# Attention plus SwiGLU on one core: odd output tiles paired into one group of seven products, output groups side by side, two weight sums later

## The chip, the cores and the metric

The kernel runs on one core of a Trainium2 chip. The metric is device time in microseconds (us) from the first to the last instruction of an execution. The kernel before takes 407.28 us (median of three runs, 407.09 to 407.64). A profiled execution of it has a span of 405.0 us; a profile's span is not a timed run, so below spans are compared with spans and times with times. A **slot** is the time from the start of one matmul to the start of the next when nothing is waited for; a **hole** is what a start comes later than its slot. The **ramp** is what runs before the first group of the first output stage, the **tail** what runs from the start of the last product to the end.

## The reference, cut to what matters

```python
# q, k, v: (8, 12, 448, 64) float32; w_gate, w_val: (768, 1536); w_out: (1536, 768)
scores = scale * np.matmul(q, k.transpose(0, 1, 3, 2)) - np.log(S)
attn = 1.0 / (1.0 + np.exp(-scores))                 # a sigmoid, no softmax
attn_out = np.matmul(attn, v)
x = attn_out.transpose(0, 2, 1, 3).reshape(B * S, H * D)     # (3584, 768)
g = x @ w_gate
silu = g * (1.0 / (1.0 + np.exp(-g)))
val = x @ w_val
out = silu * val @ w_out                                     # (3584, 768)
```

## The kernel before

The eight batches go through the feed-forward part in four pairs, `pb` = 0 to 3 (`LAST` is 3). Each pair has a first-layer stage, which makes twelve tiles `hT` (hidden channels by tokens), and an output stage, which multiplies them with `w_out`. A pair has 896 tokens, seven output tiles of 128 (`m` = 0 to 6). In tiles 0 to 5, tile `g` and tile `g + 3` form **group** `g`. A group is calculated in the manner of Strassen: seven products of six matmuls instead of eight, paid for with sums of the inputs (`S`, made on VectorE from `hT`) and of the weights (`w_sum` for the output layer, `fast_w` for the first). Tile 6 has no partner and takes the ordinary 24 matmuls. `double` is the same trick for two channel tiles of the first layer; half of pair 2's first layer and all of pair 3's use it.

A group has two PSUM banks (pieces of the memory in which TensorE collects its results). A "snap" copies a bank, scaled, to the output tile while the bank goes on collecting; a "put" adds a bank to what the output tile holds. Each product is numbered as in the code; the order is 1, 2, 6, 5, 7, 3, 4.

```python
def make_sums(most):
    for _ in range(min(most, len(sumq))):
        pb, i, f, kind = sumq.pop(0)
        ...                                            # S sums on VectorE, 128x384
        nc.vector.tensor_tensor(out=t, in0=a, in1=b, op=op)
...
def ffn2_group(pb, g):                                 # tiles g and g+3
    D = Banked("o")                                    # two PSUM banks
    ...
    mm(1, 0, True, False)                              # product 1 into bank 0
    snap(0, o1, 0)                                     # VectorE
    mm(2, 1, True, True)
    put(1, o1, 0)
    ...
    mm(6, 0, False, False)                             # bank 0 goes on: needs the snap done
    snap(0, o1, 1)
    mm(5, 1, True, False)                              # bank 1 anew: needs the put done
    o2 = osp.tile([128, DM], FP32, tag="osb", name="osb")
    snap(1, o2, 1)
    mm(7, 0, False, False)
    put(0, o2, 1)
    ...
    mm(3, 1, False, True)
    put(1, o1, 1)
    mm(4, 0, False, True)
    if not end:
        store((nc.sync, nc.sync), pb, g, o1, both)
        snap(0, o2, 0)
        store((nc.sync, nc.sync), pb, g + 3, o2, both)
        return
    ...
def ffn2(pb, m):                                       # one tile alone: 24 matmuls of 128x384
    ...
# order of the work of a pair
    extra = {
        (LAST - 1, 0): ((1, 2), (1, 4)), (LAST, 0): ((3, 3), (3, 1)), (LAST, 2): ((3, 2), (3, 4)),
    }.get((pb, f), ())                                 # fast_w sums inside `double`
    ...
    o_units = [(0.0, make_sums, (99,)), (FU2, ffn2, (pb, C - 1))]      # the odd tile comes first
    if pb == 0:
        ts = [(0.0, w_sum, (s, kind)) for s in range(2) for kind in (3, 2, 1, 4)]
        o_units += ts[:4] + [(FU2, ffn2, (pb, 0))] + ts[4:7] + [(FU2, ffn2, (pb, 3))] + ts[7:]
    for g in range(1 if pb == 0 else 0, 3):
        o_units.append((FU3, ffn2_group, (pb, g)))
```

Matmuls of the groups have line L571 in the kernel before, those of the odd tile L629, those of `double` L437. The snap is L582, the put L588, the sum S L530, `fast_w` L384 and `w_sum` L498. L460 is the addition on VectorE by which `double` empties a bank.

## Time and profile before

| | before |
|---|---|
| time, median of 3 runs | 407.28 us |
| span of the profile | 405.0 us |
| TensorE busy | 392.5 us, 97%, 3140 matmuls |
| VectorE, ScalarE, GpSimd busy | 66%, 56%, 23% |
| holes in the places that the change touches (worked out below) | 1.83 us |

An engine's timeline lists groups of like instructions: start and duration in us, engine and line, operation, output<-inputs, sizes, count; a bracket holds the idle time before them and what ended it. The prediction shows TensorE's side of three holes. Here is VectorE's side of two of them. First, beside the first group of the first output stage:

```profile
112.85 1.00 DVE L498 TENSOR_TENSOR ramp_a<-wo,ramp_a 128x1152 f16<-128x1152 f16 x1
113.77 0.55 DVE L582 TENSOR_SCALAR osb<-ps_D 128x384 f32<-128x384 f32 x1
```

The weight sum of 1.00 us stands ahead of the snap L582, and TensorE's product 6 waits for that snap. Second, the same timeline at the begin of the first `double`:

```profile
281.22 0.75 DVE L384 TENSOR_TENSOR stg_a<-wg,stg_a 128x1152 f16<-128x1152 f16 x1
281.89 1.15 DVE L460 TENSOR_TENSOR small<-ps_D,snap 128x448 f32<-128x448 f32 x2
```

The first line is a weight sum that stands ahead of L460, which releases a bank. A reader who only looks at VectorE's share of 66% would say that it has time enough. It does, but in both pairs of lines it works in the order of the program, and a sum that nobody wants yet delays an eviction that TensorE does want.

### The profile page before, as it was taken

The numbers are of one execution on the slowest core, as the hardware profiler recorded it, in microseconds if no ns is written. First come the engines' busy times: TensorE is split into PE (matmuls) and PEld (weight loads), VectorE is DVE, ScalarE is ACT, GpSimd is POOL, SyncE is SP. The second block draws the span as 40 slices with busy tenths as digits, with TensorE's granted clock in tenths as the row PEclk, the third lists the DMA queues.
The fourth block names the chain that finished last, engine by engine and source line by source line (L and its number), as shares of the span: only waits on it lengthen the run. The fifth ranks groups of instructions, "written<-read, shape, count | busy, mean of one in ns | idle before, by whom it ended". The sixth has DMA issues, their size and how long they took to land.

```text
span 405.0 us, 7990 instructions
## 1 busy us (share of the span) xinstructions
PE 392.5 (97%) x3140; PEld 203.8 (50%) x3140; DVE 266.5 (66%) x508; ACT 226.9 (56%) x355; POOL 93.7 (23%) x121
## 2 busy tenths in 40 slices
PE   6799999999999999999999999999999999999995
PEld 3444544445555444444455554444555655555563
DVE  3737556678765555567764566889786558777753
ACT  5965885744444777777764547776650035666100
POOL 4528041424222232232200120000006950000000
PEclk9999999999999999999999999999999999999999
DMA  8999989899869997778717697000001440000135
GB/s 275 245 251 249 241 189 209 166 168 237 148 187 253 241 245 160 160 159 160 160 24 189 144 248 103 2 2 1 2 0 40 121 113 0 1 2 0 40 91 143
DMA packets 65284, 54.38 MB, mean 134 GB/s; under 512 B 35744, under 2 KB 61440, under 8 KB 65248
## 3 DMA queue, kind: packets, MB, share of 16 engines
q1 hardware_dynamic: 49744, 38.22, 39.3%
q0 software_dynamic: 15072, 15.34, 23.0%
q8 instruction: 24, 0.39, 0.4%
q10 hardware_dynamic: 432, 0.33, 0.3%
q14 instruction: 12, 0.10, 0.1%
HBM read 47.19 MB, written 11.01 MB: 144 GB/s over the span
## 4 chain that ended last, share of the span: by engine, by line
PE 90%; DVE 4%; DMA 3%; ACT 1%; issue 1%; SPq 0%; POOL 0%; DVEq 0%; ACTq 0%
PE ps_D L314 34%; PE ps_D L571 18%; PE ps_D L437 15%; PE ps_D L240 8%; PE ps_D L273 8%; PE ps_D L629 6%; DMA v<-in_v_dram 2%; DMA st<-in_q_dram 1%; DVE t L336 1%; DVE xT L293 1%; DVE xT L288 0%; PE ps_D L210 0%; ACT small L467 0%; DVE stg_a L384 0%; ACT snap L447 0%
## 5 line engine op out<-in xcount | busy, mean ns | idle before, releaser
L259 ACT ACTIVATE pt_a<-ps_D 128x896 f16<-128x896 f32 x148 | 127.2, 920 | 55.3 <-PE ps_D L240 49.2
L314 PE MATMUL ps_D<-xT,wg 128*128 128x448 f16 x360 | 79.4, 353 | 0.6 <-DVE t L336 0.5
L314 PE MATMUL ps_D<-xT,wv 128*128 128x448 f16 x360 | 78.9, 352 | 0.0
L191 POOL CAST c<-stg_a 128x896 bf16<-128x896 f32 x40 | 37.5, 945 | 130.8 <-DMA stg_a<-in_q_dram 118.4
L336 DVE TENSOR_TENSOR t<-ps_D,s 128x448 f16<-128x448 f32 x60 | 37.4, 623 | 43.7 <-ACT s L334 42.6
L314 PEld LDWEIGHTS <-wg 128*128 128x128 f16 x360 | 32.3, 98 | 39.4 <-issue 13.6
L314 PEld LDWEIGHTS <-wv 128*128 128x128 f16 x360 | 35.1, 98 | 33.0 <-issue 0.4
L334 ACT ACTIVATE s<-ps_D 128x448 f16<-128x448 f32 x60 | 33.1, 551 | 26.5 <-PE ps_D L314 26.5
L240 PE MATMUL ps_D<-T,T 64*64 64x448 bf16 x644 | 44.1, 357 | 2.1 <-DVE T L216 1.2
L447 ACT ACTIVATE snap<-ps_D 128x448 f32<-128x448 f32 x54 | 28.0, 542 | 31.8 <-DVE osb L582 20.7
L340 DVE SCALAR_TENSOR_TENSOR hT<-ps_D,t 128x448 f16<-128x448 f32 x60 | 37.5, 625 | 6.3
L273 PE MATMUL ps_D<-pt_a,v 64*64 64x448 f16 x672 | 35.9, 349 | 0.6 <-DMA v<-in_v_dram 0.6
L582 DVE TENSOR_SCALAR osb<-ps_D 128x384 f32<-128x384 f32 x43 | 24.0, 557 | 18.7 <-PE ps_D L571 18.5
L571 PEld LDWEIGHTS <-S 128*128 128x128 f16 x264 | 25.8, 98 | 17.7 <-issue 0.7
L571 PE MATMUL ps_D<-ramp_a,S 128*128 128x384 f16 x198 | 34.0, 326 | 0.5 <-DVE osb L582 0.5
L588 DVE SCALAR_TENSOR_TENSOR osb<-ps_D,osb 128x384 f32<-128x384 f32 x33 | 18.4, 557 | 13.4 <-PE ps_D L571 13.3
L240 PEld LDWEIGHTS <-T 64*64 64x64 bf16 x644 | 14.9, 105 | 24.5 <-issue 17.8
L273 PEld LDWEIGHTS <-v 64*64 64x64 f16 x672 | 19.4, 107 | 13.4 <-DMA v<-in_v_dram 1.0
L571 PEld LDWEIGHTS <-hT 128*128 128x128 f16 x198 | 19.0, 98 | 14.0 <-issue 1.8
L288 DVE CAST xT<-ps_D 128x448 f16<-128x448 f32 x21 | 13.1, 624 | 19.1 <-PE ps_D L273 17.4
L629 PE MATMUL ps_D<-wo,hT 128*128 128x384 f16 x144 | 24.6, 326 | 0.2 <-DVE hT L482 0.2
L437 PE MATMUL ps_D<-xS,wv 128*128 128x448 f16 x108 | 23.4, 352 | 0.3 <-DVE small L460 0.2
(98 smaller groups left out, 426.7 us busy)
## 6 DMA issues: line engine op xcount, KB each, us to landing
out_dram<-osb SPq DMA_DIRECT2D x52, 192.0 KB, 3.0
stg_a<-in_q_dram SPq DMA_DIRECT2D x18, 448.0 KB, 5.2
stg_a<-in_k_dram SPq DMA_DIRECT2D x18, 448.0 KB, 6.0
v<-in_v_dram POOLq DMA_DIRECT2D x24, 224.0 KB, 6.0
wg<-in_moe_w_gate_dram POOLq DMA_DIRECT2D x4, 576.0 KB, 11.9
wv<-in_moe_w_val_dram POOLq DMA_DIRECT2D x4, 576.0 KB, 12.9
wo<-in_moe_w_out_dram POOLq DMA_DIRECT2D x4, 576.0 KB, 10.1
stg_a<-in_q_dram POOLq DMA_DIRECT2D x3, 448.0 KB, 13.8
```

The lines of the kernel that those rows point to most:

```text
L191: eng.tensor_copy(out=t.rearrange("p c h d -> p h c d"), in_=st.rearrange("p h (c d) -> p h c d", c=C))
L240: nc.tensor.matmul(out=sc[w * 64:(w + 1) * 64, h2, :S], lhsT=kt[r, w * 64:(w + 1) * 64], rhs=qt[r, :, w * 64:(w + 1) * 64], start=True, st ...
L259: nc.scalar.activation(out=pt, in_=sc[:, :, :S], func=SIGM, bias=sbias, scale=qkscale)
L273: nc.tensor.matmul(out=P[g:g + 64, h2, :S], lhsT=vt[r, h2, c * D:(c + 1) * D], rhs=pt[r, h2, :], start=(c == 0), stop=(c == C - 1),)
L314: nc.tensor.matmul(out=D.t[:, i, :S], lhsT=(wg16, wv16)[i][f // FW][:, pr, cs], rhs=xT[(b, pr)], start=(pr == 0), stop=(pr == NP - 1),),
L334: D.read(nc.scalar.activation(out=s16, in_=D.t[:, 0, :S], func=SIGM), 0)
L336: D.read(nc.vector.tensor_tensor(out=t1, in0=D.t[:, 0, :S], in1=s16, op=MULT), 0)
L340: nc.vector.scalar_tensor_tensor(out=hT[(b // 2, f)][:, b % 2, :], in0=D.t[:, 1, :S], scalar=hsc(b // 2), in1=t1, op0=MULT, op1=MULT),
L437: nc.tensor.matmul(out=D.t[:, bank, :S], lhsT=W(f, j), rhs=X(j), start=(start and j == 0), stop=(stop and j == JT - 1), skip_group_check=True,
L447: D.read(nc.scalar.mul(out=o, in_=D.t[:, bank, :S], mul=scale), bank)
L571: nc.tensor.matmul(out=D.t[:, bank, :hw], lhsT=l, rhs=B_(i), start=(first and i == 0), stop=(i == HF - 1), skip_group_check=True,),
L629: nc.tensor.matmul(out=D.t[:, half, :hw], lhsT=h[:, m * 128:(m + 1) * 128], rhs=wo16[f // FW][:, f % FW, half * hw:(half + 1) * hw], start ...
```

## The change

Its intent has four parts.

- The odd tiles of pairs 2 and 3 become one more group of seven products (`g == 3`), run in the last stage: 42 matmuls instead of 48. ScalarE keeps pair 2's last 128 tokens of each `hT` (`keep_rest`, 12 copies), and GpSimd makes the sums (`rest_sums`, 24 of them).
- With the odd tile gone from the head of the stage, nothing would cover the sums S. So groups 0 and 1 of pairs 2 and 3 run side by side, product by product, with their first snap on ScalarE.
- Two weight sums come later: `w_sum(1, 4)` behind the put of product 2 of the first group, `fast_w(0, 4)` into the first `double`. `fast_w(1, 4)` moves on by one `double`.
- The S sums are sorted by kind, and the first tile's store comes right after product 3's put.

```diff
     def make_sums(most):
+        if most > NF:
+            sumq.sort(key=lambda s: s[3] % 3 if s[3] < 4 else 3)
...
+    def keep_rest():
+        for f in range(NF):
+            nc.scalar.copy(out=rest_h(f), in_=hT[(LAST - 1, f)].rearrange("p b s -> p (b s)")[:, (C - 1) * 128:])
+
+    def rest_sums():
+        G.tensor_copy(out=held[:, :1], in_=hS[(LAST, 4, FW - 1)][:, :1])
+        of = lambda f: hT[(LAST, f)].rearrange("p b s -> p (b s)")[:, (C - 1) * 128:]
+        for kind in (1, 2, 3, 4):
+            for i in range(HF):
...
+                G.tensor_tensor(out=t, in0=a, in1=b, op=op)
+
-    def ffn2_group(pb, g):
+    def ffn2_group(pb, g, act=False):
...
+        rows = ((pb, g), (pb, g + 3)) if g < 3 else ((LAST - 1, C - 1), (LAST, C - 1))
...
         mm(1, 0, True, False)
-        snap(0, o1, 0)
+        if act:
+            D.read(nc.scalar.mul(out=o1[:, :hw], in_=D.t[:, 0, :hw], mul=1.0 / hsc(pb)), 0)
+        else:
+            snap(0, o1, 0)
+        yield
         mm(2, 1, True, True)
         put(1, o1, 0)
...
         mm(3, 1, False, True)
         put(1, o1, 1)
+        if not end:
+            store((nc.sync, nc.sync), *rows[0], o1, both)
+        yield
         mm(4, 0, False, True)
         if not end:
-            store((nc.sync, nc.sync), pb, g, o1, both)
             snap(0, o2, 0)
...
+    def ffn2_groups(pb, gs, extra=()):
+        gens = [ffn2_group(pb, g, len(gs) > 1) for g in gs]
+        extra = list(extra)
+        while gens:
+            gens = [g for g in gens if next(g, g) is not g]
+            if extra:
+                extra.pop(0)()
...
-                (LAST - 1, 0): ((1, 2), (1, 4)), (LAST, 0): ((3, 3), (3, 1)), (LAST, 2): ((3, 2), (3, 4)),
+                (LAST - 1, 0): ((0, 4), (1, 2)), (LAST - 1, 2): ((1, 4),), (LAST, 0): ((3, 3), (3, 1)), (LAST, 2): ((3, 2), (3, 4)),
...
-        o_units = [(0.0, make_sums, (99,)), (FU2, ffn2, (pb, C - 1))]
+        o_units = [(0.0, make_sums, (99,))]
+        if pb < LAST - 1:
+            o_units.append((FU2, ffn2, (pb, C - 1)))
...
+        ex = {(0, 1): (lambda: None, lambda: w_sum(1, 4)), (LAST - 1, 0): (keep_rest,)}
+        gs = {0: ((1,), (2,)), LAST - 1: ((0, 1), (2,)), LAST: ((0, 1), (3,), (2,))}.get(pb, ((0,), (1,), (2,)))
+        for g in gs:
+            o_units.append((FU3 * len(g), ffn2_groups, (pb, g, ex.get((pb, g[0]), ()))))
```

More of the change, by code (lines that the diff above doesn't have):

```diff
@@ L541, in store_half, with h_of @@
         eng.dma_start(out=d, in_=osb[w * 64:(w + 1) * 64, cols])
-    def ffn2_group(pb, g):
+    rest_h = lambda i: pt_f[:, 5 * JT * FW * 128 + i * 128:5 * JT * FW * 128 + (i + 1) * 128]
+    rest_s = lambda i: half_of(stg_a)[:, i * 128:(i + 1) * 128]
+    def keep_rest():
[6 more added lines that the diff above has]
+            for i in range(HF):
+                f = i // FW * 2 * FW + i % FW
+                hS[("rest", kind, i)] = t = rest_s((kind - 1) * HF + i)
+                a, b, op = {
+                    1: (of(f), of(f + FW), ADD), 2: (rest_s(i), rest_h(f), SUB), 3: (rest_h(f), of(f), SUB),
+                    4: (rest_h(f + FW), rest_s(HF + i), SUB),
+                }[kind]
+                G.tensor_tensor(out=t, in0=a, in1=b, op=op)
+    def ffn2_group(pb, g, act=False):
         D = Banked("o")
         cs = slice(g * 128, (g + 1) * 128)
-        def h_of(f, m):
+        rows = ((pb, g), (pb, g + 3)) if g < 3 else ((LAST - 1, C - 1), (LAST, C - 1))
+        def h_of(f, r):
             f1 = lambda i: i // FW * 2 * FW + i % FW + f
+            p, m = rows[r]
+            if p != pb:
+                return lambda i: (rest_h(f1(i)), None)
             return lambda i: (hT[(pb, f1(i))].rearrange("p b s -> p (b s)")[:, m * 128:(m + 1) * 128], f1(i))
         def s_of(kind):
+            if g == 3:
+                return lambda i: (hS[("rest", kind, i)], None)
             return lambda i: (hS[(pb, kind, i)][:, cs], None)
@@ L561, in ffn2_group @@
         prods = {
-            1: (h_of(0, g), w_of(0, 0)), 2: (h_of(FW, g), w_of(1, 0)), 3: (s_of(4), w_of(1, 1)),
-            4: (h_of(FW, g + 3), t_of(4)), 5: (s_of(1), t_of(1)), 6: (s_of(2), t_of(2)), 7: (s_of(3), t_of(3)),
+            1: (h_of(0, 0), w_of(0, 0)), 2: (h_of(FW, 0), w_of(1, 0)), 3: (s_of(4), w_of(1, 1)),
+            4: (h_of(FW, 1), t_of(4)), 5: (s_of(1), t_of(1)), 6: (s_of(2), t_of(2)), 7: (s_of(3), t_of(3)),
         }
@@ L597, in ffn2_group @@
         if end:
-            store((nc.sync, nc.sync), pb, g, o1, lo)
+            store((nc.sync, nc.sync), *rows[0], o1, lo)
+        yield
         mm(6, 0, False, False)
         snap(0, o1, 1)
+        yield
         mm(5, 1, True, False)
@@ L603, in ffn2_group @@
         snap(1, o2, 1)
+        yield
         mm(7, 0, False, False)
@@ L606, in ffn2_group @@
         if end:
-            store((nc.sync, nc.sync), pb, g + 3, o2, hi)
+            store((nc.sync, nc.sync), *rows[1], o2, hi)
+        yield
         mm(3, 1, False, True)
         put(1, o1, 1)
+        if not end:
+            store((nc.sync, nc.sync), *rows[0], o1, both)
+        yield
         mm(4, 0, False, True)
         if not end:
-            store((nc.sync, nc.sync), pb, g, o1, both)
             snap(0, o2, 0)
-            store((nc.sync, nc.sync), pb, g + 3, o2, both)
+            store((nc.sync, nc.sync), *rows[1], o2, both)
             return
-        store((nc.sync, nc.scalar), pb, g, o1, hi)
+        store((nc.sync, nc.scalar), *rows[0], o1, hi)
         oe = stg_tile().rearrange("p a b -> p (a b)")
         snap(0, oe, 0)
-        store((nc.sync, nc.scalar), pb, g + 3, oe, lo)
+        store((nc.sync, nc.scalar), *rows[1], oe, lo)
+    def ffn2_groups(pb, gs, extra=()):
[5 more added lines that the diff above has]
+                extra.pop(0)()
     def ffn2(pb, m):
@@ L668 @@
             tt += FU4
-        o_units = [(0.0, make_sums, (99,)), (FU2, ffn2, (pb, C - 1))]
+        o_units = [(0.0, make_sums, (99,))]
+        if pb < LAST - 1:
+            o_units.append((FU2, ffn2, (pb, C - 1)))
         if pb == 0:
             ts = [(0.0, w_sum, (s, kind)) for s in range(2) for kind in (3, 2, 1, 4)]
-            o_units += ts[:4] + [(FU2, ffn2, (pb, 0))] + ts[4:7] + [(FU2, ffn2, (pb, 3))] + ts[7:]
-        for g in range(1 if pb == 0 else 0, 3):
-            o_units.append((FU3, ffn2_group, (pb, g)))
+            o_units += ts[:4] + [(FU2, ffn2, (pb, 0))] + ts[4:7] + [(FU2, ffn2, (pb, 3))]
+        ex = {(0, 1): (lambda: None, lambda: w_sum(1, 4)), (LAST - 1, 0): (keep_rest,)}
+        gs = {0: ((1,), (2,)), LAST - 1: ((0, 1), (2,)), LAST: ((0, 1), (3,), (2,))}.get(pb, ((0,), (1,), (2,)))
+        for g in gs:
+            o_units.append((FU3 * len(g), ffn2_groups, (pb, g, ex.get((pb, g[0]), ()))))
         units += o_units
@@ L899 @@
             xs2 = [f for j in range(NJ) for f in x_sums(LAST - 1, j)]
-            w2 = [lambda a=a: fast_w(*a) for a in ((1, 3), (1, 1), (0, 3), (0, 1), (0, 2), (0, 4))]
+            w2 = [lambda a=a: fast_w(*a) for a in ((1, 3), (1, 1), (0, 3), (0, 1), (0, 2))]
             h = NF // 2
@@ L904 @@
                 (-2, h + 5, xs2[6:9]), (-1, h, xs2[9:]), (-1, h + 2, w2[2:3]), (-1, h + 3, w2[3:4]),
-                (-1, h + 4, w2[4:5]), (-1, h + 5, w2[5:]),
+                (-1, h + 4, w2[4:]),
             ):
@@ L914 @@
             early_w(2)
+        if fn is make_sums and (LAST, 4, FW - 1) in hS and ("rest", 1, 0) not in hS:
+            rest_sums()
 _INS = ['q', 'k', 'v', 'moe_w_gate', 'moe_w_val', 'moe_w_out']
```

## The prediction

> **What bounds the kernel now.** I read the page first: busy shares and the chain that ended last.
>
> ```profile
> PE 392.5 (97%) x3140; PEld 203.8 (50%) x3140; DVE 266.5 (66%) x508; ACT 226.9 (56%) x355; POOL 93.7 (23%) x121
> ...
> PE 90%; DVE 4%; DMA 3%; ACT 1%; issue 1%; SPq 0%; POOL 0%; DVEq 0%; ACTq 0%
> ```
>
> TensorE is busy for 97% of a 405.0 us span and carries 90% of the chain; no other engine passes 66%. So the time is the sum of matmul slots plus the few holes between them. A matmul taken away pays its slot, a hole pays its length, and work on VectorE, ScalarE or GpSimd costs nothing unless it opens a hole. Next I cut the span into stages (columns: stretch, its length, then busy us and instruction count per engine, clock, DMA):
>
> ```profile
> 279.00:303.20 24.20, 23.89 (x126) 12.18 (x125) 19.65 (x43) 14.77 (x30) 0.00 (x0) 1.00 0.01 1
> 303.20:307.70 4.50, 4.29 (x27) 2.27 (x25) 3.27 (x10) 0.75 (x2) 0.99 (x2) 1.00 0.00 0
> 307.70:328.20 20.50, 20.50 (x128) 12.35 (x127) 11.70 (x21) 0.49 (x1) 20.26 (x23) 1.00 0.37 97
> ...
> 375.80:379.70 3.90, 3.90 (x26) 2.35 (x24) 3.28 (x10) 0.76 (x2) 0.00 (x0) 1.00 0.01 4
> 379.70:400.40 20.70, 20.68 (x128) 12.23 (x125) 11.72 (x21) 0.49 (x1) 0.00 (x0) 1.00 0.41 107
> ```
>
> The two odd output tiles (24 matmuls each) are the stretches that begin at 303.2 and 375.8; the three groups of seven products follow each. The groups are full. The 303.2 stretch lasts 4.50 where its twin takes 3.90, so it holds a hole. VectorE and ScalarE are light there (11.7 and 0.5 us in 20.5), which is the room that the change uses. Holes then come from the timeline of TensorE (start, length, instruction; the bracket is idle time and its releaser):
>
> ```profile
> 111.77 2.12 PE L571 MATMUL ps_D<-wo,hT 128*128 128x384 f16 x12
> ...
> 114.37 3.09 PE L571 MATMUL ps_D<-ramp_a,S 128*128 128x384 f16 x18 [0.47 <-DVE osb L582]
> ```
> ```profile
> 281.04 1.30 PE L437 MATMUL ps_D<-xS,stg_a 128*128 128x448 f16 x6
> 282.56 1.29 PE L437 MATMUL ps_D<-xS,wv 128*128 128x448 f16 x6 [0.22 <-DVE small L460]
> 283.69 1.30 PE L437 MATMUL ps_D<-xS,stg_a 128*128 128x448 f16 x6
> ```
> ```profile
> 303.24 0.81 PE L629 MATMUL ps_D<-wo,hT 128*128 128x384 f16 x4
> 304.26 3.59 PE L629 MATMUL ps_D<-wo,hT 128*128 128x384 f16 x20 [0.21 <-DVE hT L482]
> ```
>
> Durations overlap (modelled ends), so I use start to start: undisturbed groups give 126 matmuls in 20.49 us, that is 0.1626 us per 128x384 matmul, and six 128x448 matmuls take 1.14 us. By that measure the holes are 114.37 − 111.77 − 12×0.1626 = 0.65; 282.56 − 281.04 − 1.14 = 0.38, followed by 285.08 − 283.69 − 1.14 = 0.25 on a ScalarE snap that the same delay made late; and 304.26 − 303.24 − 4×0.1626 = 0.37 us.
>
> **What the Trainium skill says.** "TensorE: Matmul & The Clock Gate", section "Wait — 56ns, not 53.3ns?", gives N ÷ 2.4 GHz plus about 2.5 ns from start to start on a warm array: 162.5 ns for N = 384. The trace agrees: 162.6 ns. "Perfetto Trace Analysis", section "Identifying the Most-Contended Engine", warns that matmul busy share is no measure of distance from the roofline. Here it bears on the method: I use the gaps between starts, not the 97%. "SBUF — State Buffer", section "SBUF: two separate sides", says that a VectorE operation with two SBUF inputs and a GpSimd operation that reads SBUF exclude each other: the later one blocks. The trace agrees:
>
> ```profile
> 103.27 0.98 POOL L191 CAST c<-stg_a 128x896 bf16<-128x896 f32 x1 [1.40 <-DMA stg_a<-in_k_dram]
> ```
> ```profile
> 103.37 1.48 DVE L498 TENSOR_TENSOR ramp_a<-wo 128x1152 f16<-128x1152 f16 x1
> 104.78 0.75 DVE L498 TENSOR_TENSOR ramp_a<-wo,ramp_a 128x1152 f16<-128x1152 f16 x1
> ```
>
> The sum that began 0.10 us after the cast took 1.48 us instead of 0.75: almost exactly the rest of the cast (0.88) more.
>
> **The change, part by part.**
>
> (A) Six fewer matmuls. The two odd tiles, 2×24 = 48 matmuls of 128x384, become one group of 7×6 = 42. Saved: 6×0.1626 = 0.98 us.
>
> (B) The 0.37 us hole at 304.26. The old odd tile needed hT_4, written by the last pair just before, as its fifth matmul. The side-by-side groups start with 12 matmuls that need older tiles only; hT_4 is the 14th, 13×0.1626 = 2.1 us after 303.24. VectorE delivers it by about 304.2. Saved: 0.37.
>
> (C) One of the two weight sums, (0,4), leaves the end of the ordinary stage and goes behind the two L460 additions on VectorE. Before, its 0.75 us run ended at 281.97 and L460 started at 281.89. Now L460 can start at about 281.2, its first half ends near 281.8, and product 5 may begin on time at 282.18. The ScalarE chain (snap, two silu, snap) starts on the heels of L460. In later pairs the needed snap ends about 3.24 us after the start of product 6 and is read at 3.40; here I expect it at 3.4, so about 0.05 is left. Saved: 0.38 + 0.25 − 0.05 = about 0.6.
>
> (D) The other sum, (1,4) of the output weights, at 112.85 to 113.85, stood ahead of the group's first snap. It moves behind the put of product 2. The snap then runs at about 112.95 to 113.50 and product 6 starts on time at 113.73: 0.65 gained. But the sum now runs from about 114.45 to 115.2, and the snap of product 6 behind it ends at about 115.76, while product 7 wants that bank at 113.73 + 12×0.1626 = 115.68. About 0.15 comes back as a small wait. Net 0.5.
>
> (E) Added, meant to be hidden. 12 copies of 128x128 on ScalarE (estimate from its 0.49 us for 384 and 0.54 for 448 columns: about 0.28 each, 3.4 us) in a stretch of 20 us where it is idle. GpSimd gets 24 sums of 128x128: 0.91 us for 384 columns and 1.03 for 448 extrapolate to about 0.44, or 0.23 by their start-to-start spacing, so 5.5 to 10.6 us. It can do four before the last pair ends, the rest from about 377.2, and is done by 386 at worst. In the old clock, the first of them is wanted at 375.84 + 96×0.1626 = 391.4. VectorE swaps two half-tile copies for seven group evictions of 0.56 us. All off the path.
>
> (F) Side by side. The 24 matmuls of products 1 and 2 last 3.9 us, just what the odd tile lasted; so the six sums on VectorE (377.06 to 379.25 in the last stage) still end before product 6 at 379.74. The first snap is on ScalarE, so it does not queue behind those sums. Each later step has 12 matmuls (1.95 us) against two evictions (1.12 us). Gain and cost: none.
>
> Sum: 0.98 + 0.37 + 0.6 + 0.5 = 2.45 us.
>
> **Rivals.** *GpSimd blocks the last VectorE sums.* The six sums and the 24 GpSimd ones now run at the same time, both reading SBUF. If they alternate, six steps of 0.36 + 0.3 to 0.44 end at 381.2 to 382.0 instead of 379.25. The put of product 2 behind them then ends at 381.8 to 382.6, while product 5 wants its bank at 375.84 + 36×0.1626 = 381.69. That opens a hole of 0.1 to 0.9 us. For it: the pair of lines above. Against: GpSimd waits for the same last hT, and its operations are short. I take 0.2.
>
> *A wait for output buffers.* Four buffers of 128x768 serve four tiles at once. The group after the pair writes its first half into the buffer whose store was issued in the sixth step. In the trace the second half's store lands 2.8 us after an issue that lies 0.52 after the eviction's end at 314.31, so 3.35 us. From the start of the stage: eviction ends at 66×0.1626 + 0.19 + 0.56 = 11.5, landing 14.85; the snap wants it at 90×0.1626 + 0.19 = 14.82 and has until about 15.0 before product 6 feels it. On the edge, twice. I take 0.1 in all; a slower landing of 0.5 us would cost 0.7 in all.
>
> *The gains are lost elsewhere.* If earlier matmuls only met later ones waiting for data, (C) and (D) would give nothing and about 1.3 us would be left. Against: from 129 to 279 TensorE is busy for 149.5 of 150.0 us and waits for no load. *VectorE or ScalarE as the new bound*: in the stage views they are at 57% and below 20%; this would cost microseconds, but I see no place for it.
>
> **Range and chances.** 2.45 − 0.2 − 0.1 = 2.15, so 407.28 − 2.15 = 405.1 us. If everything hides, 404.7; with (D) fully repaid (0.5 less) and 0.6 of new holes, 406.1. I add the scatter of the runs, 0.3 each way, on the good side. So 404.3 to 406.2 holds 8 in 10. Two per cent is 8.1 us: no part of the change is a quarter of it. Faster by over 2%: 0.01; within: 0.98; slower: 0.01.
>
> **What would show it.** (A) Matmuls with 384 columns fall in number by 6; the last stage is 28 products of six, at 0.1626 us each, without holes. (B) No hole in the first 24 matmuls of the output stage near 303, which lasts 126×0.1626 = 20.5 us in all. (C) Product 5 of the first pair starts 1.14 us after product 6. (D) Product 6 of the first group follows product 1 by 1.95 us, then a wait of up to 0.2 before product 7. (E) TensorE never waits for GpSimd. (F) TensorE waits at product 6 or product 5 of the last side-by-side groups, if the rival of the blocked sums is right; at product 6 of the group after them, with VectorE idle before its snap, if the buffers are. The prediction is wrong if such a wait passes 1 us, or if the span falls by under 1 us though the matmuls are gone.

## The result, and the profile after

| | before | changed |
|---|---|---|
| median of 6 runs | 407.12 us (406.81 to 407.64) | 404.6 us (403.98 to 406.96) |
| ratio, 95% interval | | 0.9944 (0.9919 to 0.997) |
| span of the profile | 405.0 us | 402.4 us |
| mean granted TensorE clock in it | 0.998 | 0.999 |

A ratio here and below is the mean time of one kernel's fast runs over the mean time of the other's fast runs of the same rounds, so it is not quite the ratio of the medians in the table. The interval lies below 1.

Busy shares and chain shares on the page of the changed kernel:

```profile
PE 391.4 (97%) x3134; PEld 203.8 (51%) x3134; DVE 269.4 (67%) x509; ACT 230.5 (57%) x369; POOL 106.0 (26%) x146
...
PE 94%; DMA 3%; DVE 1%; ACT 1%; issue 0%; SPq 0%; POOL 0%; DVEq 0%; ACTq 0%
```

TensorE has six matmuls less, and its share of the chain of waits rises from 90% to 94%, while VectorE's falls from 4% to 1%: what went was waiting on VectorE. The places of the old holes on TensorE's timeline (group matmuls are L599 in this kernel):

```profile
112.20 2.12 PE L599 MATMUL ps_D<-wo,hT 128*128 128x384 f16 x12
114.16 3.09 PE L599 MATMUL ps_D<-ramp_a,S 128*128 128x384 f16 x18
117.08 1.14 PE L599 MATMUL ps_D<-wo,S 128*128 128x384 f16 x6
...
280.83 1.30 PE L437 MATMUL ps_D<-xS,stg_a 128*128 128x448 f16 x6
281.97 1.30 PE L437 MATMUL ps_D<-xS,wv 128*128 128x448 f16 x6
...
284.24 1.30 PE L437 MATMUL ps_D<-xS,wv 128*128 128x448 f16 x6
...
302.40 4.06 PE L599 MATMUL ps_D<-wo,hT 128*128 128x384 f16 x24
306.30 6.01 PE L599 MATMUL ps_D<-ramp_a,S 128*128 128x384 f16 x36
```

No line carries a bracket. The starts say the same: 114.16 − 112.20 = 1.96 for twelve matmuls, 117.08 − 114.16 = 2.92 for eighteen, 281.97 − 280.83 = 1.14 for six of 448 columns and 284.24 − 281.97 = 2.27 for the next twelve, 306.30 − 302.40 = 3.90 for 24. Each is the undisturbed slot. Two stretches of stages (length, then busy us and count for TensorE, its weight loads, VectorE, ScalarE, GpSimd; clock; DMA share and GB/s):

```profile
302.40:322.87 20.47, 20.47 (x127) 12.33 (x126) 12.92 (x28) 4.08 (x16) 17.25 (x19) 1.00 0.27 78
370.54:398.00 27.46, 27.46 (x169) 16.34 (x167) 17.91 (x35) 1.71 (x4) 8.55 (x20) 1.00 0.34 96
```

Both output stages are full from end to end. **Where the time came from**, part by part, each measured from start to start on the two timelines:

| part | before | changed | gained |
|---|---|---|---|
| A: six matmuls of 128x384 less, 0.1626 us each | 48 | 42 | 0.98 us |
| B: head of the third output stage | 0.37 + 0.18 | 0 | 0.55 us |
| C: first `double`, products 5 and 7 | 0.38 + 0.25 | 0 | 0.63 us |
| D: product 6 of the first group | 0.65 | 0 | 0.65 us |
| sum | | | 2.81 us |

The 0.18 of B is a second hole that the prediction did not count: behind 304.26 the old tile's 20 matmuls took 307.69 − 304.26 = 3.43 us, where 20 slots are 3.25. It lies at the tile's sixth matmul, which needs the next tile of `hT` and starts at 304.60, 0.34 after the fifth instead of 0.16. Two differences belong to no part. In this execution the changed kernel reached the first group at 112.20 instead of 111.77 (an early wait for a load of `v` lasted 0.94 us instead of 0.56), and its tail was 5.49 instead of 5.79 us (the spans to two places are 402.36 and 405.03). The ramp varies from execution to execution: in the traces the first group starts between 111.66 and 112.79, so a difference of 0.5 us between two spans says nothing until the starts are compared. The account is −0.43 + 2.81 + 0.30 = 2.68 us, and the spans differ by 2.67. The lowest times differ by 406.81 − 403.98 = 2.83, the medians by 2.52.

The waits that the prediction feared are seen too, but none reaches TensorE. VectorE's and GpSimd's sums at the head of the last stage (L532 is S, L563 the sums of the rest, L616 the put):

```profile
371.60 1.04 POOL L563 TENSOR_TENSOR stg_a<-hT,hT 128x128 f16<-128x128 f16 x2 [7.18 <-DVE hT L482]
...
371.77 1.08 DVE L532 TENSOR_TENSOR S<-hT,hT 128x384 f16<-128x384 f16 x2
372.60 2.93 POOL L563 TENSOR_TENSOR stg_a<-stg_a,pt_a 128x128 f16<-128x128 f16 x6
...
373.77 1.08 DVE L532 TENSOR_TENSOR S<-hT,S 128x384 f16<-128x384 f16 x2
```

Six sums take 371.77 to 374.85, 3.08 us; before they took 377.06 to 379.25, 2.19 us. They alternate with GpSimd's. The old 2.19 is not the right measure of the slowing, though: sorted by kind, a sum no longer needs the result of the one just ahead, and in the changed kernel's third stage, without GpSimd beside them, the six take 1.69 us (303.62 to 305.31). The starts of the old ones are 0.38 to 0.39 us apart where one needs the last and 0.28 where it does not. So GpSimd costs these sums about 1.4 us, and the sorting gave 0.5 back. No run undoes the sorting alone. The two puts behind them end at about 375.8; the first, at about 375.33, releases the bank of product 5, which is wanted 36 slots after 370.54, at 376.39. So there was one microsecond to spare. And VectorE waits for an output buffer, a little:

```profile
317.33 0.56 DVE L610 TENSOR_SCALAR osb<-ps_D 128x384 f32<-128x384 f32 x1 [0.52 <-DMA out_dram<-osb]
...
318.00 3.09 PE L599 MATMUL ps_D<-ramp_a,S 128*128 128x384 f16 x18
```

Of the 0.52 us idle, 0.42 is the wait for TensorE that VectorE has ahead of the other snaps of this stage too, so the buffer delays the snap by about 0.10. It ends at 317.89; product 6, due at 318.00, starts on time. In the last stage it is the same (0.51 us idle, end at 386.02, product 6 at 386.14), though the profile names TensorE as the last releaser there.

One thing nobody had asked for is new. The third stage is one tile shorter, so the last pair's first `double` now meets GpSimd's weight sums, of which the last three begin at 325.60:

```profile
325.95 1.18 DVE L384 TENSOR_TENSOR g<-wv 128x1152 f16<-128x1152 f16 x1
327.17 1.35 DVE L384 TENSOR_TENSOR wv<-wv,wg 128x1152 f16<-128x1152 f16 x1
```
```profile
325.60 3.69 POOL L384 TENSOR_TENSOR pt_a<-wg,pt_a 128x384 f16<-128x384 f16 x3
```

Before, the same two VectorE sums took 0.75 and 0.76 us and the three GpSimd sums 2.65, because GpSimd was done at 329.56 and VectorE began at 331.25. No hole follows on TensorE.

### The profile page after: what moved, and what is told of

Its sections match the earlier page's. It is cut to its first block, busy times and chain, and to the rows that moved or that the text cites.

```text
span 402.4 us, 8032 instructions
## 1 busy us (share of the span) xinstructions
PE 391.4 (97%) x3134; PEld 203.8 (51%) x3134; DVE 269.4 (67%) x509; ACT 230.5 (57%) x369; POOL 106.0 (26%) x146
## 4 chain that ended last, share of the span: by engine, by line
PE 94%; DMA 3%; DVE 1%; ACT 1%; issue 0%; SPq 0%; POOL 0%; DVEq 0%; ACTq 0%
PE ps_D L314 35%; PE ps_D L599 20%; PE ps_D L437 18%; PE ps_D L240 8%; PE ps_D L273 8%; PE ps_D L675 4%; DMA v<-in_v_dram 2%; DMA st<-in_q_dram 1%; PE ps_D L210 0%; DVE t L336 0%; DVE xT L288 0%; DVE xT L293 0%; DVE T L216 0%; ACT s L334 0%; ACT pt_a L259 0%
## 5 line engine op out<-in xcount | busy, mean ns | idle before, releaser
L599 PEld LDWEIGHTS <-S 128*128 128x128 f16 x264 | 25.8, 98 | 17.1
L599 PE MATMUL ps_D<-ramp_a,S 128*128 128x384 f16 x198 | 33.6, 326 | 0.0
L616 DVE SCALAR_TENSOR_TENSOR osb<-ps_D,osb 128x384 f32<-128x384 f32 x36 | 20.0, 557 | 13.8 <-PE ps_D L599 13.8
L599 PEld LDWEIGHTS <-hT 128*128 128x128 f16 x204 | 19.6, 98 | 14.5 <-issue 1.8
L293 DVE CAST xT<-ps_D 64x448 f16<-64x448 f32 x37 | 23.0, 622 | 0.8
```

The lines of the kernel that those rows point to most:

```text
L599: nc.tensor.matmul(out=D.t[:, bank, :hw], lhsT=l, rhs=B_(i), start=(first and i == 0), stop=(i == HF - 1), skip_group_check=True,),
```

## The experiments

Theory: TensorE's slots set the time, so each removed slot and each closed hole is worth its length, and nothing else moves the time. Rivals: the gains would meet other waits and not add up (then undoing one part would give back less than its hole); GpSimd's sums or the output buffers cost something that hides in the sum. The profile's start-to-start times decide, because timed runs of one kernel scatter by up to 0.7% (403.98 to 406.96 us for the changed kernel), which is 3.0 us.

### The odd tile behind the pair, or ahead of it

Both keep the groups side by side and the later weight sums, and take the fourth group away. The first puts the odd tile behind the two groups, the second ahead of them, as before.

```diff
-        ex = {(0, 1): (...), (LAST - 1, 0): (keep_rest,)}
-        gs = {..., LAST - 1: ((0, 1), (2,)), LAST: ((0, 1), (3,), (2,))}
+        ex = {(0, 1): (...)}
+        gs = {..., LAST - 1: ((0, 1), (2,)), LAST: ((0, 1), (2,))}
         for g in gs:
             o_units.append(...)
+            if pb >= LAST - 1 and len(g) > 1:                  # e1 only
+                o_units.append((FU2, ffn2, (pb, C - 1)))
...
-        if pb < LAST - 1:
+        if True:                                               # e2 only
             o_units.append((FU2, ffn2, (pb, C - 1)))
```

> Everything of the change stays, but the two odd tiles are again two tiles of 24 matmuls each, placed behind the side-by-side groups; no copies on ScalarE and no sums on GpSimd for them. My theory: only the six matmuls come back, 6 x 0.1626 = 0.98 us, so the stretch from the first output matmul of a stage to its last grows by 0.98 us over both stages together and the span is about 403.4 against 402.4 of the changed kernel. Rival (the gain came from the order or from the waits, not from the matmul count): the span stays within 0.3 us of 402.4.

> As the run before, but the odd tiles of 24 matmuls come first, ahead of the side-by-side groups, as in the kernel before. My theory: 0.98 us for the matmuls, and the hole after the fourth matmul of the third output stage returns with the 0.55 us that it has in the trace of before (0.37 for the fifth matmul, 0.18 for the sixth), because the fifth and sixth matmul need tiles that VectorE has not finished. Span about 404.0, and 0.5 to 0.6 us above the run with the odd tiles behind. Rival (that hole was chance or was moved, not removed): the two runs agree within 0.2 us.

Measured: spans of 403.4 and 403.7 us, medians of four runs 406.25 (405.18 to 407.36; ratio 0.9984, 0.9955 to 1.0014) and 406.03 (405.52 to 406.74; ratio 0.998, 0.9962 to 0.9998), the kernel before at 406.81 in the same rounds. TensorE in the first:

```profile
302.20 4.06 PE L599 MATMUL ps_D<-wo,hT 128*128 128x384 f16 x24
...
315.85 4.07 PE L675 MATMUL ps_D<-wo,hT 128*128 128x384 f16 x24
```

and in the second, whose stage begins with the odd tile:

```profile
302.26 0.81 PE L675 MATMUL ps_D<-wo,hT 128*128 128x384 f16 x4
303.30 3.60 PE L675 MATMUL ps_D<-wo,hT 128*128 128x384 f16 x20 [0.22 <-DVE hT L482]
306.73 4.06 PE L599 MATMUL ps_D<-wo,hT 128*128 128x384 f16 x24
```

In the first no hole is left: 302.20 to 326.57 is 24.37 us, 150 slots of 0.1625. Against the changed kernel it has only the six matmuls more. Its span is 1.0 longer, but that is in part chance, as the ramp is 0.2 us shorter and the tail 0.3 longer here. From the start of the first group to that of the last product it takes 397.64 − 112.00 = 285.64 us, the changed kernel 396.87 − 112.20 = 284.67: part A is worth its 0.98. In the second the holes of part B are back: 303.30 − 302.26 − 4×0.1626 = 0.39 and 306.73 − 303.30 − 20×0.1626 = 0.18, together 0.57. Its last product starts at 398.27, 0.63 later than the first's (397.64), and its first group had started 0.06 later (112.06 and 112.00), which leaves the same 0.57. So B is worth 0.55 or a little more, not 0.37. The timed rounds are the miss here: they can't tell the two apart, and their order is even the wrong way round. Two of the four timed runs of the first are 2 us longer than the other two, at clocks of 0.996 and 1.000; no trace of a long one was kept.

### One group after another

```diff
-        gs = {..., LAST - 1: ((0, 1), (2,)), LAST: ((0, 1), (3,), (2,))}
+        gs = {..., LAST - 1: ((0,), (1,), (2,)), LAST: ((0,), (1,), (3,), (2,))}
```

> The seven-product group for the odd tiles stays; the first two groups of the last two output stages are again one after the other, with the first snap on VectorE. My theory: the 24 matmuls of products 1 and 2 of the pair cover VectorE's six sums in place of the odd tile; with 12 they do not. In the third stage the sums end 2.91 us after the first output matmul, the snap 0.56 later, product 6 wants the bank at 1.95: a hole of about 1.5 us. In the last stage the sums end at 4.3 us (GpSimd slows them), so a hole of about 3.0 us. Span about 402.4 + 4.5 = 406.9. Rival (side by side is only tidiness, the sums are hidden anyway): under 0.5 us.

Measured: span 406.4, median 408.53 (408.16 to 410.13), ratio 1.0053 (1.0027 to 1.0079). It is 0.5% slower than the kernel before (the interval lies above 1), though it has six matmuls less. TensorE at the head of the last stage:

```profile
371.50 2.11 PE L599 MATMUL ps_D<-wo,hT 128*128 128x384 f16 x12
376.53 0.65 PE L599 MATMUL ps_D<-ramp_a,S 128*128 128x384 f16 x3 [2.92 <-DVE osb L610]
```

The hole is 376.53 − 371.50 − 1.95 = 3.08 us. In the third stage, the same two lines start at 301.86 and 305.31: 1.50 us. That is as expected (3.0 and 1.5). VectorE's six sums stand ahead of the first snap, and with twelve matmuls ahead of product 6 instead of 24 there is nothing to hide them. The odd tile was work, but also cover; running two groups side by side, with the first snap on ScalarE, is what makes part A pay.

### The weight sums back at their old places

```diff
-                (LAST - 1, 0): ((0, 4), (1, 2)), (LAST - 1, 2): ((1, 4),), ...
+                (LAST - 1, 0): ((1, 2), (1, 4)), ...
...
-            o_units += ts[:4] + [(FU2, ffn2, (pb, 0))] + ts[4:7] + [(FU2, ffn2, (pb, 3))]
-        ex = {(0, 1): (lambda: None, lambda: w_sum(1, 4)), (LAST - 1, 0): (keep_rest,)}
+            o_units += ts[:4] + [(FU2, ffn2, (pb, 0))] + ts[4:7] + [(FU2, ffn2, (pb, 3))] + ts[7:]
+        ex = {(LAST - 1, 0): (keep_rest,)}
...
-                (-1, h + 4, w2[4:]),
+                (-1, h + 4, w2[4:5]), (-1, h + 5, w2[5:]),       # and (0, 4) again in w2
```

> Only the two weight sums go back to their old places; the rest of the change stays. My theory: the holes of 0.65 us in the first output stage and of 0.38 + 0.25 us in the first pair of the third stage return whole, 1.28 us, span about 403.7. Rival (matmuls that come earlier only wait longer for later data): the two holes return but the span grows by under 0.4 us.

Measured: span 403.2, median 405.14 (404.68 to 405.42), ratio 0.9956 (0.9941 to 0.9971). TensorE:

```profile
112.06 2.12 PE L599 MATMUL ps_D<-wo,hT 128*128 128x384 f16 x12
114.41 1.78 PE L599 MATMUL ps_D<-ramp_a,S 128*128 128x384 f16 x10 [0.23 <-DVE osb L610]
...
282.61 1.29 PE L437 MATMUL ps_D<-xS,wv 128*128 128x448 f16 x6 [0.22 <-DVE small L460]
```

C comes back whole: the product ahead of 282.61 starts at 281.09, and 282.61 − 281.09 − 1.14 = 0.38, with 0.25 behind it. D comes back as 114.41 − 112.06 − 1.95 = 0.40 instead of 0.65. VectorE tells why:

```profile
113.13 0.76 DVE L498 TENSOR_TENSOR ramp_a<-wo,ramp_a 128x1152 f16<-128x1152 f16 x1
```

The sum took 0.76 us here and 1.00 in the kernel before. In the kernel before, GpSimd was casting when it ran; here GpSimd's cast of 111.90 was over before the sum began at 113.13. In both the sum began 1.07 us after product 1. So 0.25 of the old hole came from how a sum and a cast happened to lie, and the place of the sum gives the other 0.40. Together 1.03 us came back (0.63 + 0.40), where 1.28 were expected. The span is only 0.87 longer (403.23 and 402.36) because the ramp was 0.14 shorter here (112.06 against 112.20). That part of the 0.65 which depends on the cast is not the change's own merit alone.

### The first snap on VectorE, with GpSimd's sums at the same time or later

In the first, only the place of the first snap is undone. In the second GpSimd's sums begin after VectorE's last sum as well.

```diff
     def ffn2_groups(pb, gs, extra=()):
-        gens = [ffn2_group(pb, g, len(gs) > 1) for g in gs]
+        gens = [ffn2_group(pb, g, False) for g in gs]
...
     def rest_sums():                                           # e6 only
-        G.tensor_copy(out=held[:, :1], in_=hS[(LAST, 4, FW - 1)][:, :1])
+        G.tensor_copy(out=held[:, :1], in_=hS[(LAST, 4, HF - 1)][:, :1])
```

> The changed kernel with one edit: the first snap of each side-by-side group is on VectorE again, behind its six sums. This makes the end of the sums visible to TensorE. In the third stage they end 2.9 us after the first output matmul, two snaps fit before product 6 at 3.9: no hole. In the last stage they end at 4.3 us, because GpSimd's sums hold them up (1.08 us per two instead of 0.62): my theory is one hole of 0.9 to 1.0 us at product 6 of the last stage, and none in the third. Rival (the order on VectorE alone causes it, GpSimd has no part): a hole of the same size in both stages, or in neither.

> As the run before, and in addition GpSimd's 24 sums start only when VectorE's last sum is written. My theory: the six sums of the last stage take about 1.9 us instead of 3.1, the snap is ready in time and the hole of 0.9 to 1.0 us is gone; TensorE still never waits for GpSimd. Rival (GpSimd has no part in it): the hole stays as in the run before.

Both were run for one look, with a profile. The first took 406.27 us, span 404.5; the second 404.73, span 402.9 (the kernel before 406.9 on that chip). In the first, the last two of VectorE's six sums (the first began at 373.20) and product 6 of the last stage:

```profile
374.99 1.07 DVE L532 TENSOR_TENSOR S<-hT,S 128x384 f16<-128x384 f16 x2
...
376.58 0.65 PE L599 MATMUL ps_D<-ramp_a,S 128*128 128x384 f16 x3 [0.97 <-DVE osb L610]
```

and in the second, the first two sums, GpSimd's first, and product 6:

```profile
372.65 0.62 DVE L532 TENSOR_TENSOR S<-hT,hT 128x384 f16<-128x384 f16 x2
...
374.55 1.58 POOL L563 TENSOR_TENSOR stg_a<-hT,hT 128x128 f16<-128x128 f16 x4
...
375.03 1.14 PE L599 MATMUL ps_D<-ramp_a,S 128*128 128x384 f16 x6
```

With GpSimd's sums out of the way the six VectorE sums take 372.65 to 374.35, 1.70 us instead of 2.86. The first kernel's hole is 376.58 − 371.55 − 3.90 = 1.13 us (24 slots; 0.97 of it is listed as idle). In the second it is gone: 375.03 − 371.13 = 3.90. In the third stage, where GpSimd makes no such sums then, the first of the two kernels has no hole either (306.75 − 302.85 = 3.90). This shows two things. GpSimd's sums are what slows VectorE's. And the ScalarE snap is what keeps that slowness off TensorE; it is worth 1.13 us as long as the two run together, and nothing if GpSimd begins later.

The first kernel had a second hole that I had not expected, of 0.56 us, near 330. The VectorE weight sum, which took 1.18 us beside GpSimd's in the changed kernel, took 2.91:

```profile
326.41 2.91 DVE L384 TENSOR_TENSOR g<-wv 128x1152 f16<-128x1152 f16 x1
```

Here VectorE waited for all three GpSimd sums; in the seven other runs in which it met two of them or more (the changed kernel and its repetition, the early sums, the late GpSimd sums, the three on the output buffer) it took turns with them. What decides is open: the VectorE sum began 0.37 us into a GpSimd sum here, and 0.35 in the changed kernel. So the new clash of the changed kernel can cost 0.56 us. Whether it does so in some of its timed runs is the next but one question.

### The wait for the output buffer

The first edit gives the snap that waits a place of its own, the second was to give it the next buffer of the pool, and the third makes the wait longer on purpose, by putting the store of the first tile behind product 4.

```diff
-        o1 = osp.tile([128, DM], FP32, tag="osb", name="osb")
+        follows = (pb, g) in ((LAST - 1, 2), (LAST, 3))               # e7
+        if follows:
+            o1 = pt_f[:, 7296:7296 + 2 * DM].bitcast(FP32)
+        else:
+            o1 = osp.tile([128, DM], FP32, tag="osb", name="osb")
...
+        if (pb, g) in ((LAST - 1, 2), (LAST, 3)):                     # e8, instead
+            osp.tile([128, DM], FP32, tag="osb", name="skip")
...
-        if not end:                                                   # e10, instead
+        swap = act and g == 0
+        if not end and not swap:
             store((nc.sync, nc.sync), *rows[0], o1, both)
         yield
         mm(4, 0, False, True)
+        if swap:
+            store((nc.sync, nc.sync), *rows[0], o1, both)
```

> The changed kernel with one edit: the group that follows the side-by-side pair writes its first tile into a buffer of its own, so it waits for no store. My theory: VectorE's idle time of 0.52 and 0.51 us ahead of that snap, released by the store's landing, is gone and the snap starts about 0.1 us earlier; TensorE has no hole in either kernel, so the output stages keep their length within 0.05 us. Rival (the wait costs time): the stages get shorter by 0.1 us or more.

> The opposite: one buffer is skipped, so that snap waits for the store of the second group of the pair, which is issued about 1 us later. My theory: the store lands about 318.5 in the clock of the changed kernel's trace, the snap ends near 319.1 and product 6, wanted at 318.0, is late by 1.1 to 1.5 us, in both of the last stages: span 404.6 to 405.4. Rival (there is more slack in the buffers than the trace shows): under 0.3 us per stage.

> The run with a skipped buffer changed nothing (its snap waits for the same store as before, so it was no test). Here the stores of the pair's two first tiles swap places in the queue, so that the one whose buffer is reused lands later: it is issued about 1.0 + 1.2 us later, lands near 17.2 us after the stage's first matmul, the snap that wanted it at 14.8 ends near 17.8 and product 6, wanted at 15.6, starts late. My theory: a hole of 1.9 to 2.3 us in both of the last stages, span 406.2 to 407.0; so the early store is needed and has no slack to give. Rival: there is slack, under 0.5 us per stage.

The own place: 404.49 us, span 402.7. The snap now waits for TensorE alone:

```profile
317.55 0.56 DVE L610 TENSOR_SCALAR pt_a<-ps_D 128x384 f32<-128x384 f32 x1 [0.42 <-PE ps_D L599]
```

and the products follow one another at 316.37 and 318.32, 1.95 apart, just as they do in the changed kernel at 316.05 and 318.00. The wait of the changed kernel costs nothing. The next buffer: 404.31, span 402.5, and no hole, but it is a miss. In its trace the snap has the same waits as in the changed kernel, TensorE and the store that is first in the queue; the edit changed nothing that could be tested. The swapped store: 405.9, span 404.1, with

```profile
318.26 0.56 DVE L610 TENSOR_SCALAR osb<-ps_D 128x384 f32<-128x384 f32 x1 [1.50 <-DMA out_dram<-osb]
318.87 2.44 PE L599 MATMUL ps_D<-ramp_a,S 128*128 128x384 f16 x14 [0.76 <-DVE osb L610]
```

a hole of 0.93 us (product 1 starts at 315.99; 318.87 − 315.99 − 1.95), and 0.90 in the last stage (385.06 to 387.91). I had expected 1.9 to 2.3 each. The snap waits for the store that stands first in the queue; that is now the other group's, which is one product of 0.98 us later, not two. A store that lands 0.98 later and a hole of 0.90 to 0.93 put the slack of the changed kernel at 0.05 to 0.08 us. That is an inference, but it agrees with the 0.11 between the snap's end at 317.89 and product 6 at 318.00: in the swapped run, where product 6 does wait, it starts 0.05 after the snap's end, which leaves 0.06. So the prediction's "on the edge, twice" was right about the edge, and the changed kernel stands on its good side.

### The clash of weight sums, and the scatter

In the result's six runs of the changed kernel one took 406.96 us. To see whether the clash near 326 is the cause, the VectorE sums were spread over later `double`s; the changed kernel was run again beside it, five rounds each.

```diff
-                ..., (LAST, 0): ((3, 3), (3, 1)), (LAST, 2): ((3, 2), (3, 4)),
+                ..., (LAST, 2): ((3, 3), (3, 1)), (LAST, 4): ((3, 2),), (LAST, 6): ((3, 4),),
```

> The changed kernel unaltered, for its scatter (403.98 to 406.96 us in six runs) and beside the next run. The traces show a clash that the prediction did not see: the third output stage is one odd tile shorter, so GpSimd's weight sums for the last stage now end about 3 us after VectorE has begun its own weight sums in the first pair of that stage, and both slow down (VectorE 1.18 and 1.35 us instead of 0.75; in one run 2.91, with a hole of 0.56 us on TensorE). If this is the cause of the scatter, some runs here are 0.5 us longer at full clock; if it is the clock, long runs have a clock under 1.0.

> The changed kernel, with VectorE's four weight sums of the last stage moved one to three pairs later, where GpSimd is idle. My theory: the first pair of the last stage is free of the clash, GpSimd's last three sums take 2.65 us again, no run has the hole of 0.56 us; since the profiled run of the changed kernel just fits, the profiled span stays at 402.4 within 0.3, and the mean of the timed runs is 0 to 0.4 us lower. Rival (the clash costs nothing on average): the same mean and scatter as the changed kernel.

Measured: the changed kernel again has a median of 404.49 (403.87 to 405.15), ratio 0.9928 (0.9908 to 0.9947), span 402.5; with the sums spread it is 404.54 (404.12 to 405.46), ratio 0.993 (0.9911 to 0.9948), span 402.7. The kernel before had a median of 407.08 in these rounds. In the spread version the clash is gone: the two VectorE sums run at 334.27 and take 0.75 and 0.76 us, and GpSimd's last three, at 325.96, take 2.65 us again. The time is the same. So no cost of the clash is seen in these six runs each, and nothing shows that the scatter comes from it. The run of 406.96 had a mean granted clock of 0.990, the lowest of its rounds. That is not the whole cause of scatter: the kernel before has six runs of 406.64 to 407.08 and five of 408.0 to 408.7 in these rounds, all at clocks of 0.995 to 1.000. What makes them differ is open. The five also pull the ratios here below 0.994; the medians differ by 2.59 us, much as in the first rounds (2.52).

### The same for the odd tiles of pairs 0 and 1

If a pair of odd tiles is worth 0.98 us, the other pair should be as well. On top of the spread sums of the run above, this edit keeps pair 0's rest in free columns of a weight buffer, sums it with pair 1's, and takes the odd tile out of both stages.

```diff
-        if pb < LAST - 1:
-            o_units.append((FU2, ffn2, (pb, C - 1)))
+        if pb == 0:
+            o_units.append((0.0, keep_rest, (0,)))
...
-        gs = {0: ((1,), (2,)), LAST - 1: ...
+        gs = {0: ((1,), (2,)), 1: ((0, 1), (2,), (3,)), LAST - 1: ...
```

> The lesson carried on: with the spread sums of the run above, the odd tiles of the first two output stages are paired as well, in a group of seven products at the end of the second stage (copies on ScalarE, sums on GpSimd into buffer columns that are free by then). My theory: six more matmuls go, 0.98 us, if no hole opens; profiled span 401.4 within 0.4. Rival (the first two stages run beside the attention steps: GpSimd's 9 us of sums hold up its casts, or the six sums of the first stage lose their cover): a hole of 0.5 us or more there, and the span is not below 402.0.

This failed. The result is wrong (relative error 5.2), the median 410.14 (409.64 to 414.79), ratio 1.0089. I did not find the cause of the wrong result; a buffer read after its contents were replaced is a guess. Its profile (span 408.4) has a hole near 102 to 105, where no odd tile covers VectorE's work any more and four weight sums stand ahead of an eviction (105.25 − 102.22 − 11×0.1626 = 1.24 us), and more waits between 277 and 298, where attention's steps had slipped. Nothing follows about the idea, except that in this form it loses its cover as the "one after another" kernel did.

## Why the prediction was right, and where its sizes were off

The prediction was right: 404.6 us against 405.1, inside 404.3 to 406.2. It was 0.5 us too high, and its steps show where.

- **The bound.** "A matmul taken away pays its slot, a hole pays its length." Shown: six matmuls paid 0.98 (the odd tile behind the pair), and A to D add up to 2.81 where the spans, the ramp and the tail account for 2.8. Nothing was lost on the way, so the rival "the gains are lost elsewhere" fell.
- **(A)** 0.98, right.
- **(B)** The step "Saved: 0.37" was too small; it measured 0.55 (0.57 in the kernel with the odd tile first). I counted the hole that had a bracket, at the fifth matmul, and took the twenty matmuls from there as full, though their listed duration, 3.59, could not tell; start to start they took 3.43 instead of 3.25, with a second hole at the sixth. My own method, applied one line further, would have shown it.
- **(C)** "About 0.05 is left" measured 0: 0.63 instead of 0.6. The kernel with the early sums gave 0.38 and 0.25 back.
- **(D)** "About 0.15 comes back as a small wait" was wrong; product 7 started on time, and D is 0.65, not 0.5. In the changed kernel the sum runs at 114.83 and the snap behind it at 115.50, ending at 116.05; the bank is wanted at 116.11. I had stacked durations end to end, but a VectorE operation starts 0.08 to 0.09 before the listed end of the one ahead (114.36 + 0.56 = 114.92 against 114.83; 114.83 + 0.75 = 115.58 against 115.50). Two such steps, and a first put that ended where I had put it, decided 0.15 us. What the experiment adds: 0.25 of the 0.65 hole was a GpSimd cast beside the sum.
- **(E)** Right as to cost: ScalarE's twelve copies took 2.48 us (I said 3.4), GpSimd's 24 sums were done at 380.15, where the first of them is wanted at 386.14, and TensorE never waits for GpSimd.
- **(F)** Right, and shown by taking it away: without the two groups side by side the change loses 1.50 + 3.08 us.
- **Rival, blocked sums** (0.2 taken): the mechanism is there, 3.08 us for six sums instead of 1.69 in the third stage. It cost nothing. My line "while product 5 wants its bank at 375.84 + 36×0.1626 = 381.69" was right; the estimate that the put would end at 381.8 at the earliest was too late. Moved to the new clock (minus 5.30), the put was to end at 376.5 or later and ended at 375.33. I let each pair of operations take 0.66 to 0.80 us; the six sums measured 0.51 each. Moving the snap back to VectorE turns the same slowness into 1.13 us.
- **Rival, output buffers** (0.1 taken): VectorE is idle for 0.52 and 0.51 us, of which the store accounts for about 0.10; TensorE waits for none of it. The working had the right wait and the right edge: the snap was to start 14.85 us after the stage's first matmul, and started at 317.33 − 302.40 = 14.93.
- **Range.** 2.81 less nothing, instead of 2.45 less 0.3, is 0.66 us lower than 405.1, at 404.5; the median was 404.6. All errors (B, C, D and the 0.3 taken for the rivals) have one sign, so nothing cancelled by luck. Two ends of the range do not come out of the prediction's own terms: 2.45 − 0.5 − 0.6 leaves 405.9 and not 406.1, and 0.3 below 404.7 is 404.4 and not 404.3.
- **Three readings to put right.** The pair of lines under "SBUF — State Buffer" shows 1.48 − 0.75 = 0.73 us more, not "almost exactly" the 0.88 that the cast still had to run; the sum is held up, but it ends 0.15 earlier than waiting for the cast's listed end and then 0.75 would give. The shares "57% and below 20%" hold for the stretches of the groups; in the stretch from 279.00 to 303.20, where (C) lies, VectorE is busy for 19.65 of 24.20 us, 81%, and ScalarE for 61%. It did not matter, as no new hole opened there. And the 162.5 ns that it takes from the Trainium skill is an estimate, worked out from the formula on the page "TensorE: Matmul & The Clock Gate"; the trace has 162.6.

## What to carry to other kernels

Where one engine is busy for 97%, count its holes from start to start, every one of them, also behind the line that carries the bracket; each one closed and each slot removed then paid its full length here. Before removing work from that engine, ask what the work was covering: the odd tile hid the sums and their eviction, and taking it out alone made the kernel slower, until two groups side by side gave 24 matmuls of cover and the first eviction went to an idle engine. An in-order queue delays what is urgent by what is not, so put sums that nobody wants yet behind the evictions, and remember that a shorter stage moves the idle engines' work against other work.

## What the Trainium skill lacked or had wrong

- "SBUF — State Buffer", section "SBUF: two separate sides": the clashes looked at here agree with its exclusive lock. What the page lacks is who wins in a sequence. A VectorE sum of 128x1152 beside three consecutive GpSimd sums of 128x384 took 1.18 us when the two took turns (the changed kernel) and 2.91 us when it waited for all three (the kernel with the snap on VectorE), against 0.75 alone; which of them happens is worth 0.56 us on TensorE.
- "Perfetto Trace Analysis", section "DVE / Act Engine Instruction (TENSOR_ADD, Activation, etc)": its listed window runs to the acknowledged write, while the next instruction may begin to read earlier. The trace agrees. The section gives no size; a later one, "Optimizing Scalar/DVE Operations", names an overhead of about 60 ns on SBUF and 125 ns on PSUM and says that as much again overlaps with the next instruction. Here most consecutive VectorE operations of 384 to 1152 columns overlap by 0.08 to 0.09 us, with inputs in PSUM and in SBUF alike. The error of stacking durations end to end was 0.15 us in (D).
- "GPSIMD Engine Reference", section "3.1 Elementwise — side-by-side cycle accounting": its measured time is for 2048 columns of float32, its rate is about 2.6 cycles for each element (an estimate of 2.2 ns at the 1.2 GHz that the section uses), and it gives no fixed cost in time. Here, undisturbed, start to start, a two-input fp16 sum of 384 columns took 0.87 us (2.60 for three, the kernel before) and one of 128 columns 0.39 us (9.28 for all 24, the run with the late GpSimd sums), so 1.9 ns for each column and about 0.15 us fixed.
